# One pass over the weight rows for Q, K and V of an octet, with held stationary rows for K and V

## The chip, the cores and the metric

The kernel runs on one core of a Trainium2 chip. The time is device microseconds of one execution; 2,165.54 us is the median of three runs before (2,163.02 to 2,171.04). Engines are named as in the profile: PE (matrix multiply), with its weight loads on a track of their own (PEld), DVE (vector), ACT (scalar), POOL and SP (SyncE, which only issues transfers here). "Clock" is the share of full speed that PE's clock was granted.

## The reference

Two parts are mixed by a gate. Part B is a gated MLP over 2,048 rows; it takes the first 350 us and the change leaves it alone. Part A is what this case is about: 64 segments of 32 rows, each with 8 memory rows in front, and each segment's memory is the output of the one before, so the segments run one after another.

```python
# D = 640, H = 32 heads of 192, M = 8 memory rows, seg = 32
for s in range(64):
    h = concat([mem, x[s*32:(s+1)*32]])          # 40 rows
    q, k, v = h @ Wq, h @ Wk, h @ Wv             # 640 -> 32 * 192 each
    p = softmax(mask(q @ k.T * 192**-0.5))       # per head
    o = (p @ v) @ Wo                             # 6144 -> 640
    mem = o[:8]; outs.append(o[8:])
return sigmoid(x @ gate_w) * concat(outs) + (1 - ...) * mlp(x)
```

## The kernel before

The weights of part A are 31.5 MB, of which the program keeps 22.6 MB in SBUF beside the rest. They are cut in 84 pieces: for each octet (8 heads, four octets) and each of five 128-row slices k one piece of Q, of K and of V (384 KB each), and 24 pieces of Wo (320 KB). 60 pieces stay in SBUF, 24 are streamed again in every segment through a ring of five slots. A table of costs spreads the streamed pieces evenly over the order in which they are used.

```python
PROG = [("q", 0), ("tq", 0), ("k", 0), ("tk", 0), ("v", 0),
        ("q", 1), ("sc", 0), ("tq", 1), ("k", 1), ("ex", 0), ("tk", 1), ("v", 1),
        ("q", 2), ("pt", 0), ("sc", 1), ("tq", 2), ("k", 2), ("ex", 1), ("tk", 2), ("pv", 0), ("v", 2),
        ("q", 3), ("pt", 1), ("sc", 2), ("tq", 3), ("k", 3), ("ex", 2), ("tk", 3), ("pv", 1), ("v", 3),
        ("wo", 0), ("pt", 2), ("sc", 3), ("ex", 3), ("pv", 2), ("wo", 1), ("wo", 2, 0), ("pt", 3), ("wo", 2, 1),
        ("pv", 3), ("wo", 2, 2), ("wo", 3)]
```

Of a segment's 40 rows the program puts 32 in a column tile of PE (`128*32` in the profile) and leaves out the last 8 positions of x; their Q and K are made for all segments in advance, their V once for four segments. PROG is the order of work of one segment, and each engine follows it with its own instructions: q, k, v are the matmuls with their evictions on ACT (PE writes into the banks of PSUM; an eviction copies a bank to SBUF, and the program lets the bank be written again only then), tq and tk the transposes of Q and K on DVE, sc the scores on PE with maximum and subtraction on DVE, ex the exponentials on ACT with sum, reciprocal and product on DVE, pt the transposes of the probabilities on PE with their evictions on DVE, pv and wo the last two products. Q or K of an octet:

```python
def cmode(s, m, o, bank):
    for k in range(KT):                                   # KT = 5
        g_, rg_ = piece(s, (m, o, k))                     # resident, or the ring slot
        S_.add("pe", [lambda e, j=j, ...: e.matmul(       # loads the 32 rows of H, then 384 columns
            ps[32*j:32*j+32, bank, 0:384]..., Hb[hb][:, k, 0:L], gv[:, j],
            start=(k == 0), stop=(k == KT-1), tile_position=(0, 32*j)) for j in range(4)], ...)
    S_.add("act", ... out=rows_sb[m], in_=ps[:, bank, 0:384] ...)      # "rows evac"
```

V (`v_oct`) has the same form. In every fourth segment (s % 4 == 0) it makes V a second time in the same loop, for the memory positions of the next four segments, into a second PSUM bank that DVE evicts. These are called double-V segments below, the others ordinary ones. Of the eight PSUM banks five (`misc_bank`) are handed out in turn; two are for scores and one for the output. V has two buffers in SBUF (`NVB = 2`).

Of the kernel before, what the change touches and what calls it, by code (L numbers as in the profile page):

```python
# [3 lines left out]
ACTF = mybir.ActivationFunctionType  # L4
# [217 lines left out]
def _build(nc, A_x, A_mem0, A_Wq, A_Wk, A_Wv, A_Wo, seg_len, w_gate, w_up, w_down,  # L222
           gate_w, out, opts=None):
# [5 lines left out]
    L = int(seg_len)  # L229
    assert Bsz == 1 and M == 8 and L == 32 and Dh == 192  # L230
    assert Dm % 128 == 0 and H % 4 == 0 and S % 128 == 0 and Df % 128 == 0
    KT = Dm // 128
# [8 lines left out]
    XA = L - M  # L241
# [15 lines left out]
    S_ = _Sched(nc)  # L257
# [26 lines left out]
    NVB, NUB = 2, 2  # L284
# [34 lines left out]
    ps = nc.alloc_psum_tensor("ps", [128, 8, 512], F32)  # L319
# [5 lines left out]
    o = wsA_base - wsB_total  # L325
# [6 lines left out]
    o = wsA_base  # L332
# [4 lines left out]
    o = ffn_base  # L337
# [14 lines left out]
    Hb = [bview(o_H + b * KT * R * 2, KT * R * 2).rearrange("p (k r) -> p k r", r=R) for b in range(2)]  # L352
    r_Hm = [sreg(o_H + b * KT * R * 2, 8) for b in range(2)]
    r_Hxp = [sreg(o_H + b * KT * R * 2 + 8, KT * R * 2 - 8) for b in range(2)]
    o_Hx = wsA_off["Hx"]
    Hx = bview(o_Hx, KT * 256).rearrange("p (k t) -> p k t", t=128)
    r_Hx = sreg(o_Hx, KT * 256)
# [26 lines left out]
    rows_sb = [bview(wsB_off["rows"] + b * 768, 768) for b in range(2)]  # L384
    r_rows = [sreg(wsB_off["rows"] + b * 768, 768) for b in range(2)]
# [3 lines left out]
    v_sb = [bview(wsB_off["v"] + b * 768, 768) for b in range(NVB)]  # L389
# [69 lines left out]
    def piece_view(key, o):  # L459
        if key[0] == 3:  # L460
            return bview(o, GO).rearrange("p (c n) -> p c n", n=Dm)
        return bview(o, GQ)

    PROG = [("q", 0), ("tq", 0), ("k", 0), ("tk", 0), ("v", 0),
            ("q", 1), ("sc", 0), ("tq", 1), ("k", 1), ("ex", 0), ("tk", 1), ("v", 1),
            ("q", 2), ("pt", 0), ("sc", 1), ("tq", 2), ("k", 2), ("ex", 1), ("tk", 2), ("pv", 0), ("v", 2),
            ("q", 3), ("pt", 1), ("sc", 2), ("tq", 3), ("k", 3), ("ex", 2), ("tk", 3), ("pv", 1), ("v", 3),
            ("wo", 0), ("pt", 2), ("sc", 3), ("ex", 3), ("pv", 2), ("wo", 1), ("wo", 2, 0), ("pt", 3), ("wo", 2, 1),
            ("pv", 3), ("wo", 2, 2), ("wo", 3)]
    assert NOCT == 4  # L470
    WOP = 6
    COST = dict(q=0.17, k=0.17, v=0.2, sc=0.5, pt=0.2, pv=0.5, wo=0.26, tq=0.0, tk=0.0, ex=0.0)

    def wo_pairs(item):
        o_ = item[1]
# [6 lines left out]
    tt = 0.0  # L482
    for item in PROG:
        kind, i = item[0], item[1]
        if kind in ("q", "k", "v"):
            keys = [("qkv".index(kind), i, k) for k in range(KT)]
        elif kind == "wo":
            keys = [(3, p) for p in wo_pairs(item)]
        else:
            tt += COST[kind]  # L490
            continue
        for key in keys:
            order.append(key)
            tcons.append(tt)
            tt += COST[kind]
# [60 lines left out]
    def piece(seg, key):  # L556
        oi = order_index[key]
        assert oi == last_req.get(seg, -1) + 1, "pieces must be consumed in `order`"
        last_req[seg] = oi
        if seg == 0:  # L560
            load_late(oi + LATE)
        if key in res_off:
            assert slot_class[key] != 1 or order_index[key] <= order_index[late[late_done[0] - 1]]
            return piece_view(key, res_off[key]), r_res[key]
        issue_ring(seg, stream_pos[key])
        slot = ring_of[(seg, key)]
        return piece_view(key, ring_off[slot]), r_ring[slot]
# [7 lines left out]
            load_resident(late[late_done[0]])  # L575
            late_done[0] += 1

    left_stream = [order[i] for i in stream_list if order[i][0] < 2]
    left_slot = {}

    def issue_left(upto):
# [278 lines left out]
    def misc_bank():  # L860
        misc[0] += 1
        return misc[0] % 5
# [1 line left out]
    def apx(ap, dims):  # L864
        return bass.AP(ap.tensor, ap.offset, [list(ap.ap[0])] + [list(d) for d in dims])

    def cmode(s, m, o, bank):
        hb = s % 2
        for k in range(KT):
            g_, rg_ = piece(s, (m, o, k))  # L870
            gv = g_.rearrange("p (c j i) -> p j c i", c=12, j=4)
            S_.add("pe", [lambda e, j=j, k=k, gv=gv: e.matmul(  # L872
                ps[32 * j:32 * j + 32, bank, 0:384].rearrange("p (c i) -> p c i", i=32), Hb[hb][:, k, 0:L], gv[:, j],
                start=(k == 0), stop=(k == KT - 1), tile_position=(0, 32 * j)) for j in range(4)],
                reads=[rg_, r_Hm[hb], r_Hxp[hb]], writes=[r_ps[bank]], name="%s s%d o%d k%d" % ("QK"[m], s, o, k))
        S_.add("act", lambda e: e.activation(out=rows_sb[m], in_=ps[:, bank, 0:384], func=ACTF.Copy),  # L876
               reads=[r_ps[bank]], writes=[r_rows[m]], name="rows evac")

    def row_transp(s, m, o):
        src = rows_sb[m].rearrange("p (t c r) -> p t c r", c=3, r=L)  # L880
# [7 lines left out]
        for i, (a, lo) in enumerate(((8, 0), (12, 64))):  # L888
            S_.add("dve", lambda e, a=a, lo=lo: e.transpose(out=Ks[lo:lo + 64, a:a + 4, 0:L], in_=src[lo:lo + 64, :, 1]),  # L889
                   reads=[r_rows[1]], writes=[r_K[1 + i][0]], name="Tk s%d o%d" % (s, o))  # L890

    def v_oct(s, o):
        hb = s % 2
        bank = misc_bank()
        left = s % 4 == 0
        bank2 = misc_bank() if left else None

        def mms(bk, lhs, k, g_):
            return [lambda e, j=j: e.matmul(  # L899
                ps[32 * j:32 * j + 32, bk, 0:384], lhs, g_[:, 384 * j:384 * (j + 1)],  # L900
                start=(k == 0), stop=(k == KT - 1), tile_position=(0, 32 * j)) for j in range(4)]

        for k in range(KT):
            g_, rg_ = piece(s, (2, o, k))
            S_.add("pe", mms(bank, Hb[hb][:, k, 0:L], k, g_),
                   reads=[rg_, r_Hm[hb], r_Hxp[hb]], writes=[r_ps[bank]], name="V s%d o%d k%d" % (s, o, k))
            if left:
                S_.add("pe", mms(bank2, Hx[:, k, 4 * XA:128], k, g_),
                       reads=[rg_, r_Hx], writes=[r_ps[bank2]], name="Vl s%d o%d k%d" % (s, o, k))
        S_.add("act", lambda e: e.activation(out=v_sb[o % NVB], in_=ps[:, bank, 0:384], func=ACTF.Copy),  # L910
               reads=[r_ps[bank]], writes=[r_v[o % NVB]], name="V evac s%d o%d" % (s, o))
        if left:
            S_.add("dve", lambda e: e.tensor_copy(out=vl_sb[o], in_=ps[:, bank2, 0:384]),
                   reads=[r_ps[bank2]], writes=[r_vl[o]], name="Vl evac s%d o%d" % (s, o))

    def scores(s, o):
        bank = 5 + o % 2
# [108 lines left out]
    def segment(s):  # L1026
        g, q = s // 4, s % 4
        for item in PROG:
            kind, i = item[0], item[1]
            if kind in ("q", "k"):  # L1030
                cmode(s, "qk".index(kind), i, misc_bank())
                if kind == "k" and i == 0 and q == 0 and g > 0:
                    out_group(g - 1, misc_bank())
                if kind == "k" and i == 1:
                    if q == 0 and g > 0:
                        out_store(g - 1)
                    if q == 1 and g + 1 < NG:
                        perm_dma(lambda j: rowb[PP[j]], lambda j: rows(x2, g + 1)[j], [], r_rowbh, "rowb")
                    if q == 3 and g + 1 < NG:
                        x_group_transposes(g + 1, misc_bank())  # L1040
                if kind == "k" and i == 2:
                    if s + 1 < NSEG:
                        x_copy(s + 1)
                    if q == 3:
                        if g + 1 < NG:
                            gate_group(g + 1, misc_bank())
                        perm_dma(lambda j: rowb[PP[j]], lambda j: rows(b_scr, g)[j],
                                 [Rg("dr", 128 * g, 128 * g + 128)], r_rowbh, "rowb")
            elif kind == "tq":
                row_transp(s, 0, i)  # L1050
            elif kind == "tk":
                row_transp(s, 1, i)
            elif kind == "sc":
                scores(s, i)
            elif kind == "ex":
                softmax(s, i)
            elif kind == "v":
                v_oct(s, i)
            elif kind == "pt":
                p_transp(s, i)  # L1060
            elif kind == "pv":
                pv_oct(s, i)
            else:
                wo_part(s, item)
        O3 = ps[:, OB, 0:KT * R].rearrange("p (n r) -> p n r", r=R)
        if s + 1 < NSEG:
            nb = (s + 1) % 2
            S_.add("act", lambda e: e.activation(out=Hb[nb][:, :, XA:L], in_=O3[:, :, XA:L], func=ACTF.Copy),
                   reads=[r_ps[OB]], writes=[r_Hm[nb]], name="mem evac s%d" % s)
        S_.add("dve", lambda e: e.tensor_copy(out=aT4[:, :, q * XA:(q + 1) * XA], in_=O3[:, :, 0:XA]),  # L1070
               reads=[r_ps[OB]], writes=[r_aT4], name="aT evac s%d" % s)
        S_.add("dve", lambda e: e.tensor_copy(out=aT4[:, :, 4 * XA + q * M:4 * XA + (q + 1) * M], in_=O3[:, :, L:R]),
               reads=[r_ps[OB]], writes=[r_aT4], name="aT evac2 s%d" % s)
# [86 lines left out]
```

## Time and profile before

| | before |
|---|---|
| time | 2,165.54 us |
| steady part (from 350 us): one segment | 28.7 us |
| double-V segments / ordinary ones | 29.1 / 28.5 us |
| steady part: DMA, PE, DVE busy | 96%, 85%, 63% |
| half-clock time after 360 us | 64 us |

The length of a segment is the distance between two starts of ACT's memory eviction, of which there are 63 (line L1068 in the profile of before). The half-clock time is the sum of the trace's records with a granted clock of 0.5.

The windows view of before: length, then busy us (and instructions) of each engine, the granted clock, the DMA share and GB/s.

```profile
core 0: us, PE busy (x) PEld busy (x) DVE busy (x) ACT busy (x) POOL busy (x), PEclk, DMA share, GB/s
500.00:1000.00 500.00, 424.11 (x10525) 275.76 (x10521) 313.18 (x1042) 148.93 (x372) 74.29 (x329) 0.99 0.96 322
1000.00:1500.00 500.00, 424.78 (x10611) 282.72 (x10608) 315.06 (x1044) 146.70 (x367) 72.11 (x319) 0.98 0.96 320
```

PE is "busy" 85% of the time and DMA 96%, at 322 GB/s. Who ends PE's idle time is told by the waits view of PE, from 362 to 2,100 us: PE's line, what it waited for, us in total, times, the longest.

```profile
PE ps L872 <- DMA arena<-in_A_Wq_dram: 72.9, 121, 1.9
PE ps L992 <- DVE arena L978: 36.2, 96, 0.7
PE ps L1021 <- DVE arena L1008: 33.6, 97, 0.5
PE ps L899 <- DMA arena<-in_A_Wv_dram: 30.2, 48, 1.8
PE ps L1021 <- DMA arena<-in_A_Wo_dram: 29.4, 59, 3.0
```

L872 is Q and K, L899 is V, L1021 is Wo, L992 is PV. Weight pieces of the ring end most of it. Some lines of PE's timeline in an ordinary segment: start, length, instructions, and in brackets the idle time before.

```profile
1043.18 1.81 PE L872 MATMUL ps<-arena 128*32 128x384 bf16 x40 [0.29 <-ACT arena L1068]
1044.82 0.99 PE L899 MATMUL ps<-arena 128*32 128x384 bf16 x20
1045.63 0.99 PE L872 MATMUL ps<-arena 128*32 128x384 bf16 x20
...
1047.84 0.34 PE L899 MATMUL ps<-arena 128*32 128x384 bf16 x4
1049.94 0.35 PE L899 MATMUL ps<-arena 128*32 128x384 bf16 x4 [1.76 <-DMA arena<-in_A_Wv_dram]
```

The 40 matmuls of L872 start at 1043.18 and the next line starts at 1044.82: 1.64 us for 40, 41 ns each, although each has a weight load of its own (40 in the same stretch of PEld's timeline; 96 ns is the mean of one on the page). The bracket in the last line is a piece that came 1.76 us late.

Split by kind of segment, PE's idle time by what ended it (the waits view, one window for each segment; us per segment):

| before | DVE | ACT | DMA | sum |
|---|---|---|---|---|
| double-V segment | 1.49 | 0.30 | 1.05 | 2.84 |
| ordinary segment | 1.27 | 0.30 | 2.87 | 4.44 |

### The profile page before, as it was taken

The numbers are of one execution on the slowest core, as the hardware profiler recorded it, in microseconds if no ns is written. First come the engines' busy times: TensorE is split into PE (matmuls) and PEld (weight loads), VectorE is DVE, ScalarE is ACT, GpSimd is POOL, SyncE is SP. The second block draws the span as 40 slices with busy tenths as digits, with TensorE's granted clock in tenths as the row PEclk, the third lists the DMA queues.
The fourth block names the chain that finished last, engine by engine and source line by source line (L and its number), as shares of the span: only waits on it lengthen the run. The fifth ranks groups of instructions, "written<-read, shape, count | busy, mean of one in ns | idle before, by whom it ended". The sixth has DMA issues, their size and how long they took to land.

```text
span 2166.5 us, 92005 instructions
## 1 busy us (share of the span) xinstructions
PE 1836.7 (85%) x40326; PEld 1154.9 (53%) x40326; DVE 1231.5 (57%) x3952; ACT 618.8 (29%) x1480; POOL 274.1 (13%) x1210
## 2 busy tenths in 40 slices
PE   7999948888888888888888888888888888888887
PEld 3544425555555555555555555555555555555555
DVE  2222316666656566656666666656666666666665
ACT  2222212333232223332322223322323222323232
POOL 0000001111111111111111111111111111111111
PEclk9999979999999999999999999999999999999999
DMA  9203579999999999999999999999999999999998
GB/s 366 103 13 89 149 220 341 328 321 337 322 325 316 310 326 329 313 327 311 329 328 314 324 315 332 323 307 316 334 319 333 320 325 306 328 327 328 322 321 273
DMA packets 363391, 642.97 MB, mean 297 GB/s; under 512 B 60514, under 2 KB 231786, under 8 KB 362986
## 3 DMA queue, kind: packets, MB, share of 16 engines
q1 hardware_dynamic: 311914, 601.41, 81.6%
q10 hardware_dynamic: 51072, 35.66, 5.7%
q8 instruction: 315, 5.16, 0.9%
q14 instruction: 90, 0.74, 0.1%
HBM read 619.13 MB, written 17.83 MB: 294 GB/s over the span
## 4 chain that ended last, share of the span: by engine, by line
DMA 48%; PE 37%; DVE 9%; ACTq 3%; issue 2%; ACT 2%; SPq 0%; POOL 0%; DVEq 0%; POOLq 0%
DMA arena<-in_A_Wq_dram 19%; DMA arena<-in_A_Wo_dram 13%; DMA arena<-in_A_Wv_dram 10%; PE ps L872 9%; PE ps L1021 7%; PE ps L899 5%; DMA arena<-in_A_Wk_dram 4%; PE ps L804 3%; PE ps L742 2%; ACTq L819 2%; PE ps L739 2%; PE ps L757 2%; PE ps L992 2%; DVE arena L975 2%; DVE arena L1008 1%
## 5 line engine op out<-in xcount | busy, mean ns | idle before, releaser
L872 PE MATMUL ps<-arena 128*32 128x384 bf16 x10240 | 566.8, 331 | 119.9 <-DMA arena<-in_A_Wq_dram 77.6
L1021 PE MATMUL ps<-arena 128*128 128x40 bf16 x15360 | 472.1, 181 | 71.7 <-DVE arena L1008 35.9
L1021 PEld LDWEIGHTS ps<-arena 128*128 128x128 bf16 x15360 | 434.9, 97 | 116.8 <-DVE arena L1008 48.0
L872 PEld LDWEIGHTS ps<-arena 128*32 128x32 bf16 x10240 | 239.6, 96 | 346.5 <-DMA arena<-in_A_Wq_dram 172.1
L876 ACT ACTIVATE arena<-ps 128x384 bf16<-128x384 f32 x512 | 251.4, 491 | 552.2 <-PE ps L872 446.8
L899 PE MATMUL ps<-arena 128*32 128x384 bf16 x6400 | 333.1, 331 | 37.0 <-DMA arena<-in_A_Wv_dram 32.2
L835 POOL COPY arena<-arena 128x96 bf16<-128x96 bf16 x256 | 67.6, 264 | 1645.1 <-PE ps L931 1089.0
L899 PEld LDWEIGHTS ps<-arena 128*32 128x32 bf16 x6400 | 150.5, 97 | 175.6 <-DMA arena<-in_A_Wv_dram 82.0
L882 DVE STREAM_TRANSPOSE arena<-arena 128x384 bf16<-128x384 bf16 x256 | 146.0, 570 | 102.3 <-ACT arena L876 102.3
L975 DVE TENSOR_TENSOR arena<-ps,arena 128x320 bf16<-128x320 bf16 x256 | 125.8, 491 | 125.9 <-PE ps L973 121.9
L1002 ACT ACTIVATE arena<-ps 128x320 bf16<-128x320 f32 x256 | 110.7, 432 | 229.4 <-PE ps L994 229.4
L910 ACT ACTIVATE arena<-ps 128x384 bf16<-128x384 f32 x256 | 125.6, 491 | 161.9 <-PE ps L899 161.9
L839 POOL COPY arena<-arena 64x32 bf16<-64x32 bf16 (+1 forms) x768 | 165.7, 216 | 47.3
L959 DVE TENSOR_REDUCE arena<-ps 104x4 f32<-104x160 f32 x256 | 82.6, 323 | 150.6 <-ACT ps L957 148.6
L992 PE MATMUL ps<-arena 128*128 128x160 bf16 (+1 forms) x768 | 133.7, 264 | 39.6 <-DVE arena L978 38.0
L889 DVE STREAM_TRANSPOSE arena<-arena 64x128 bf16<-64x128 bf16 x512 | 145.5, 284 | 8.1
L957 ACT ACTIVATE ps<-ps 104x160 f32<-104x160 f32 x256 | 74.0, 289 | 233.9 <-DVE ps L947 189.0
L994 PE MATMUL ps<-arena 128*128 128x64 bf16 (+1 forms) x768 | 128.0, 206 | 2.1 <-DMA arena<-in_A_Wv_dram 1.0
L945 DVE TENSOR_REDUCE arena<-ps 104x4 f32<-104x160 f32 x256 | 81.0, 316 | 77.0 <-PE ps L931 77.0
L885 DVE STREAM_TRANSPOSE arena<-arena 128x256 bf16<-128x256 bf16 x256 | 111.4, 435 | 16.1 <-ACT arena L876 16.1
L992 PEld LDWEIGHTS ps<-arena 128*128 128x128 bf16 x768 | 73.9, 99 | 85.5 <-DVE arena L978 60.3
L1006 DVE CAST arena<-ps 64x160 bf16<-64x160 f32 x256 | 80.4, 314 | 52.5 <-PE ps L994 48.4
(79 smaller groups left out, 1719.8 us busy)
## 6 DMA issues: line engine op xcount, KB each, us to landing
arena<-in_A_Wo_dram SPq DMA_DIRECT2D x591, 320.0 KB, 4.9
arena<-in_A_Wq_dram SPq DMA_DIRECT2D x404, 384.0 KB, 5.3
arena<-in_A_Wv_dram SPq DMA_DIRECT2D x335, 384.0 KB, 5.1
arena<-in_A_Wk_dram SPq DMA_DIRECT2D x276, 384.0 KB, 5.3
left_qk_scratch<-arena ACTq DMA_DIRECT2D x16, 768.0 KB, 8.8
arena<-left_qk_scratch ACTq DMA_DIRECT2D x64, 192.0 KB, 4.5
arena<-in_A_x_dram SPq DMA_DIRECT2D x4, 640.0 KB, 15.1
ffn_b_scratch<-arena ACTq DMA_DIRECT2D x16, 160.0 KB, 1.8
```

What stands on the lines that cost most here:

```text
L839: S_.add("pool", lambda e, a=a, b=b, lo=lo, hi=hi, sa=sa: e.tensor_copy(out=Ks[lo:hi, a:b, L:R], in_=stg[lo:hi, o, 1, sa:sa + b - a]), rea ...
L872: S_.add("pe", [lambda e, j=j, k=k, gv=gv: e.matmul(ps[32 * j:32 * j + 32, bank, 0:384].rearrange("p (c i) -> p c i", i=32), Hb[hb][:, k, ...
L876: S_.add("act", lambda e: e.activation(out=rows_sb[m], in_=ps[:, bank, 0:384], func=ACTF.Copy), reads=[r_ps[bank]], writes=[r_rows[m]], na ...
L882: S_.add("dve", lambda e: e.transpose(out=Qs[:, :, 0:L], in_=rows_sb[0].rearrange("p (c r) -> p c r", r=L)), reads=[r_rows[0]], writes=[r_ ...
L885: S_.add("dve", lambda e: e.transpose(out=apx(Ks[:, 0, :], [[2 * R, 4], [R, 2], [1, L]]), in_=apx(rows_sb[1], [[96, 4], [64, 2], [1, L]])) ...
L889: S_.add("dve", lambda e, a=a, lo=lo: e.transpose(out=Ks[lo:lo + 64, a:a + 4, 0:L], in_=src[lo:lo + 64, :, 1]), reads=[r_rows[1]], writes= ...
L899: return [lambda e, j=j: e.matmul(ps[32 * j:32 * j + 32, bk, 0:384], lhs, g_[:, 384 * j:384 * (j + 1)], start=(k == 0), stop=(k == KT - 1) ...
L910: S_.add("act", lambda e: e.activation(out=v_sb[o % NVB], in_=ps[:, bank, 0:384], func=ACTF.Copy), reads=[r_ps[bank]], writes=[r_v[o % NVB ...
L975: S_.add("dve", lambda e: e.tensor_tensor(out=PTm, in0=apx(pv[:, 512:616], [[64, 2], [0, 4], [1, R]]), in1=apx(mbd, [[0, 2], [1, 4], [0, R]]),
L992: return [lambda e: e.matmul(full, v[:, e0:e0 + 128], PTm[:, ia:ib], start=True, stop=False, skip_group_check=True), lambda e: e.matmul(pa ...
L994: lambda e: e.matmul(part, vl[:, e0:e0 + 128], PTl[:, ia:ib], start=False, stop=True, skip_group_check=True)]
L1021: fns.append(lambda e, g_=g_, i=i, c=c, n=n, tl=tl, cc=cc, u=u: e.matmul(ps[:, OB, n * R:(n + 1) * R], g_[:, i, n * 128:(n + 1) * 128], u[ ...
```

## The change

Its intent: Q, K and V multiply the same 32 rows of H, so for each slice k the rows are loaded for Q only and K's and V's matmuls run on the rows that are in the array (`ldweights=False`). For that Q, K and V of an octet become one item, `qkv`, with k outermost; V's slice 0 comes last, so that V's bank is needed a little later. V's eviction becomes an item of its own, `ve`. The place of scores, of the softmax relative to K's transposes, and of the Wo pieces changes with it.

```diff
-    PROG = [("q", 0), ("tq", 0), ("k", 0), ("tk", 0), ("v", 0),
-            ("q", 1), ("sc", 0), ("tq", 1), ("k", 1), ("ex", 0), ("tk", 1), ("v", 1),
-            ...
-            ("wo", 0), ("pt", 2), ("sc", 3), ("ex", 3), ("pv", 2), ("wo", 1), ("wo", 2, 0), ("pt", 3), ("wo", 2, 1),
-            ("pv", 3), ("wo", 2, 2), ("wo", 3)]
+    PROG = [("qkv", 0), ("tq", 0), ("tk", 0), ("ve", 0),
+            ("qkv", 1), ("sc", 0), ("tq", 1), ("tk", 1), ("ex", 0), ("ve", 1),
+            ("qkv", 2), ("pt", 0), ("sc", 1), ("tq", 2), ("tk", 2), ("ex", 1), ("pv", 0), ("ve", 2),
+            ("qkv", 3), ("pt", 1), ("sc", 2), ("tq", 3), ("tk", 3), ("ex", 2), ("pv", 1), ("ve", 3),
+            ("wo", 0, 0), ("sc", 3), ("wo", 0, 1), ("pt", 2), ("ex", 3), ("wo", 0, 2), ("pv", 2),
+            ("wo", 1, 0), ("wo", 1, 1), ("pt", 3), ("wo", 1, 2), ("pv", 3), ("wo", 2), ("wo", 3)]
+    QKV = [(m, k) for k in range(KT) for m in range(3) if (m, k) != (2, 0)] + [(2, 0)]
...
+    def qkv_oct(s, o):
+        left = s % 4 == 0                                        # double-V segment
+        banks = [misc_bank() for _ in range(3)]
+        bank2 = misc_bank() if left else None
+        load_k = [None]
+        for m, k in QKV:
+            load = load_k[0] != k
+            load_k[0] = k
...                                                               # four matmuls, with or without load
+            if left and m == 2:
+                S_.add("pe", mms(bank2, Hx[:, k, 4 * XA:128], True), ...)     # second V
+                load_k[0] = None
+        for m in range(2): ...                                   # "rows evac" of Q and K on ACT
...
+    def v_evac(s, o):                                            # at the item "ve"
+        S_.add("act", ... out=v_sb[o % NVB], in_=ps[:, bank, 0:384] ...)
+        if bank2 is not None:
+            S_.add("dve", ... out=vl_sb[o], in_=ps[:, bank2, 0:384] ...)
```

Of the 16,640 loads for these matmuls 9,216 go. Since the streamed pieces are chosen from the order of use, the choice changes too: 14 of Q, K, V and 10 of Wo in place of 15 and 9.

## The prediction

> **What bounds it now.** After about 350 us the kernel repeats 64 recurrent segments, 28.7 us each (ACT's 63 memory evictions, 353.1 to 2130.9 us). In windows of 500 us DMA is 96% busy there at 320 to 324 GB/s, PE 85%, DVE 63%. A segment streams 24 weight pieces through a ring of five slots (15 of Q, K, V, 384 KB each; 9 of Wo, 320 KB), some 5 us each from issue to landing. SyncE waits for slots that PE frees, and PE for pieces: 146 us of PE idle time from 362 to 2100 us, 317 us on PE's load track (waits view). So the ring sets the pace, with DVE's chain (about 4.4 us an octet) close behind. Every fourth segment makes V twice (3.3 us more PE work), yet is only some 0.7 us longer: most PE time is hidden.
>
> **What the removed loads are worth: nothing.** In unbroken stretches 40 matmuls of Q and K start in 1.64 us (timeline): 41 ns each, 164 ns for four 384-column matmuls side by side. [...]the loads (97 ns each) are hidden. [...] Some 9,200 loads vanish; the matmuls stay 41 ns apart.
>
> **What moves.** The plan becomes 14 Q/K/V and 10 Wo pieces a segment, 8,576 KB instead of 8,640. At this trace's packet times (140 ns per 3,072 bytes, 63 ns per 1,280) that is 0.3% less DMA time, 5 us in all.
> Q, K and V end together after 15 groups (2.46 us); the first scores, and the DVE chain, come some 1.5 us later in a segment. In return DVE has Q's and K's transposes (1.6 us) to do during the exponentials, for which it waits 149 us now. Three PSUM banks are held at once, and V's eviction goes behind the exponentials and the PV eviction on ACT: octet 3's V meets octet 2's V bank, about 0.8 us of new PE wait. In the 16 double-V segments four of the five banks are held, and the second V's DVE eviction stands behind the mix (0.35 + 0.88 us) and the transposes: by hand some 2 us of PE wait in octet 1, 1 in octet 2, 3 in octet 3. Scores 3 waits about 1 us for K's transposes.
>
> **Sum.** An ordinary segment: chain about 1 us longer by hand, mostly under the DMA pace, some given back by the hidden exponentials: -0.5 to +0.5 us, times 48. A double-V segment: +2 to +4 us, times 16, about +45 us. DMA -5 us. I predict 2,200 us (+1.6%), 8 in 10 between 2,130 and 2,270. Faster by over 2%: 0.12; within 2%: 0.46; slower by over 2%: 0.42.
>
> **Right or wrong by.** Q/K/V matmuls still 41 ns apart; PE idle before them ended by V's evictions (ACT, DVE) more than by DMA; double-V segments 31 to 33 us, others near 28.5; steady DMA share 0.93 to 0.95; DVE's wait for exponentials clearly under 149 us.
>
> **What would make it wrong.** Held matmuls closer than 41 ns. DMA waits that absorb the bank waits as they absorb the second V now (then about 2,165). An order of pieces that feeds the ring better, towards the 375 GB/s seen around 330 to 340 us: 2 to 4% faster. Waits behind V's evictions that compound through the ring: 5% slower.

16 times +2 to +4 us was put at about +45, 48 times -0.5 to +0.5 at 0, DMA is -5, so +40 us on 2,165.5, put as 2,200. What stands there "by hand", the later start of scores and the 4.4 us of DVE's chain are estimates from instruction times of the trace of before (63% of 28.7 us, by four, gives 4.5). The 375 GB/s is 378 in the windows view of 330 to 340 us.

## The result, and the profile after

The changed kernel takes 2,360.68 us (median of four runs, 2,355.45 to 2,372.38); the kernel before took 2,164.28 on the same chip. The ratio is 1.0894 (95% interval 1.0839 to 1.095). All ratios here are the mean time of one kernel's fast runs over that of the kernel before in the same rounds, so they are not quite the ratios of the medians. The prediction was 2,200 us, at most 2,270.

The windows view of after, as above:

```profile
core 0: us, PE busy (x) PEld busy (x) DVE busy (x) ACT busy (x) POOL busy (x), PEclk, DMA share, GB/s
500.00:1000.00 500.00, 395.65 (x9576) 216.32 (x7333) 274.11 (x932) 125.17 (x332) 64.67 (x287) 0.92 0.88 287
1000.00:1500.00 500.00, 395.05 (x9570) 218.03 (x7339) 278.85 (x948) 125.61 (x334) 66.13 (x294) 0.92 0.88 287
```

DMA fell from 96% to 88% and from 320 to 287 GB/s, PE from 85% to 79%, and the granted clock from 0.98 to 0.92. No engine is busier. The last part can be seen on the page itself. First the page of before, its granted clock and DMA share in 40 slices of the span, in tenths; then the page of after.

```profile
PEclk9999979999999999999999999999999999999999
DMA  9203579999999999999999999999999999999998
```

```profile
PEclk9999979999998999998998998999998899999989
DMA  9104599899898989898989889898988898989888
```

The half-clock records sum to 279 us after 360 us, against 64. PE's waits view of after, from 362 to 2,300 us (L873 are matmuls on held rows, L898 those with a load, L1014 is PV, L919 and L922 are V's eviction on ACT and the second V's on DVE):

```profile
PE ps L1014 <- DVE arena L1000: 129.0, 207, 1.6
PE ps L873 <- DMA arena<-in_A_Wk_dram: 36.8, 51, 1.7
PE ps L898 <- DVE arena L922: 29.1, 15, 2.0
PE ps L942 <- DVE arena L935: 28.9, 42, 0.7
...
PE ps L873 <- ACT arena L919: 27.8, 48, 1.1
...
PE ps L873 <- DVE arena L922: 26.9, 15, 1.8
...
PE ps L898 <- ACT arena L919: 8.7, 15, 0.6
```

Four of these seven lines are waits for V's evictions, 92.5 us together; the kernel before has none of them. PV waits 129 us for DVE, 36 before. By kind of segment, PE's idle time by what ended it (the waits view, one window for each segment; us per segment):

| | length, us | PE idle: DVE | ACT | DMA | sum |
|---|---|---|---|---|---|
| double-V, before | 29.1 | 1.49 | 0.30 | 1.05 | 2.84 |
| double-V, after | 37.9 | 6.91 | 1.70 | 0.52 | 9.13 |
| ordinary, before | 28.5 | 1.27 | 0.30 | 2.87 | 4.44 |
| ordinary, after | 29.75 | 2.69 | 0.64 | 2.41 | 5.74 |

A double-V segment became 8.8 us longer, an ordinary one 1.2 us: 16 times 8.8 and 48 times 1.2 are 198 us, all of the loss. One double-V segment on PE's timeline (it starts at 953.7 us):

```profile
954.45 0.50 PE L873 MATMUL ps<-arena 128*32 128x384 bf16 x8
954.78 0.50 PE L898 MATMUL ps<-arena 128*32 128x384 bf16 x8
...
958.71 0.50 PE L873 MATMUL ps<-arena 128*32 128x384 bf16 x8
961.18 0.51 PE L898 MATMUL ps<-arena 128*32 128x384 bf16 x8 [1.97 <-DVE arena L922]
...
964.60 0.50 PE L873 MATMUL ps<-arena 128*32 128x384 bf16 x8
965.68 0.51 PE L898 MATMUL ps<-arena 128*32 128x384 bf16 x8 [0.58 <-ACT arena L919]
...
969.78 0.35 PE L898 MATMUL ps<-arena 128*32 128x384 bf16 x4
970.92 0.33 PE L873 MATMUL ps<-arena 128*32 128x384 bf16 x4 [0.80 <-ACT arena L919]
...
973.37 0.33 PE L873 MATMUL ps<-arena 128*32 128x384 bf16 x4 [1.79 <-DVE arena L922]
...
974.30 0.86 PE L898 MATMUL ps<-arena 128*32 128x384 bf16 x8
974.94 0.86 PE L873 MATMUL ps<-arena 128*32 128x384 bf16 x8
...
984.07 0.24 PE L1014 MATMUL ps<-arena 128*128 128x160 bf16 x1 [1.57 <-DVE arena L1000]
```

The first two lines give the pace: eight matmuls with held rows start at 954.45 and the next item at 954.78, 0.33 us, so again 41 ns each. Then come the waits: 1.97 us in octet 1 (second V's bank), 0.58 in octet 2 (V's bank), 0.80 and 1.79 in octet 3, and 1.57 before the PV of octet 2. Behind the waits of octet 3 the pace is half (the trace's record from 974.04 to 977.45 us has a granted clock of 0.5): the item that starts at 974.30 is followed at 974.94, eight matmuls in 0.64 us. What DVE does while PE waits in octet 1:

```profile
958.32 0.88 DVE L851 SCALAR_TENSOR_TENSOR arena<-ps,arena 128x640 bf16<-128x640 bf16 x1 [3.50 <-PE ps L846]
959.12 0.57 DVE L928 STREAM_TRANSPOSE arena<-arena 128x384 bf16<-128x384 bf16 x1
959.61 0.40 DVE L931 STREAM_TRANSPOSE arena<-arena 128x256 bf16<-128x256 bf16 x1
959.93 0.60 DVE L935 STREAM_TRANSPOSE arena<-arena 64x128 bf16<-64x128 bf16 x2
960.57 0.56 DVE L922 CAST arena<-ps 128x384 bf16<-128x384 f32 x1
```

The mix of the group before, Q's transposes, K's transposes, and only then the second V's eviction (L922), which ends at 961.13. PE goes on at 961.18.

### The profile page after: what moved, and what is told of

It is laid out like the page before. It is cut to its first block, busy times and chain, and to the rows that moved or that the text cites. A ratio compares the mean times of both kernels' runs of the same rounds, so it can differ in the third digit from the quotient of the medians.

```text
span 2353.6 us, 82743 instructions
## 1 busy us (share of the span) xinstructions
PE 1874.9 (80%) x40298; PEld 1001.3 (43%) x31110; DVE 1204.0 (51%) x3952; ACT 588.1 (25%) x1480; POOL 273.6 (12%) x1210
## 5 line engine op out<-in xcount | busy, mean ns | idle before, releaser
L873 PE MATMUL ps<-arena 128*32 128x384 bf16 x9216 | 640.8, 340 | 136.2 <-DMA arena<-in_A_Wk_dram 37.0
L898 PE MATMUL ps<-arena 128*32 128x384 bf16 x7424 | 598.8, 345 | 122.0 <-DMA arena<-in_A_Wv_dram 30.6
L898 PEld LDWEIGHTS ps<-arena 128*32 128x32 bf16 x7424 | 202.8, 99 | 867.4 <-issue 481.9
L1043 PEld LDWEIGHTS ps<-arena 128*128 128x128 bf16 x15360 | 458.9, 99 | 27.1 <-DMA arena<-in_A_Wo_dram 7.4
L911 ACT ACTIVATE arena<-ps 128x384 bf16<-128x384 f32 x512 | 223.2, 488 | 701.8 <-PE ps L898 602.6
L1014 PE MATMUL ps<-arena 128*128 128x160 bf16 (+1 forms) x768 | 147.6, 282 | 140.1 <-DVE arena L1000 135.6
L967 DVE TENSOR_REDUCE arena<-ps 104x4 f32<-104x160 f32 x256 | 81.6, 319 | 147.4 <-PE ps L953 145.9
L1014 PEld LDWEIGHTS ps<-arena 128*128 128x128 bf16 x768 | 79.2, 106 | 166.7 <-DVE arena L1000 166.7
L1016 PE MATMUL ps<-arena 128*128 128x64 bf16 (+1 forms) x768 | 139.7, 219 | 2.2 <-DMA arena<-in_A_Wq_dram 1.9
L919 ACT ACTIVATE arena<-ps 128x384 bf16<-128x384 f32 x256 | 125.8, 491 | 10.9 <-PE ps L898 10.4
L805 PE MATMUL ps<-arena 128*128 128x512 bf16 x470 | 105.3, 383 | 6.5 <-ACT arena L812 6.0
L1092 DVE CAST arena<-ps 128x120 bf16<-128x120 f32 x64 | 18.1, 283 | 177.7 <-ACT arena L1090 172.3
L953 PE MATMUL ps<-arena 128*40 128x40 bf16 x4096 | 96.7, 180 | 13.0 <-DVE arena L935 13.0
```

The lines of the kernel that those rows point to most:

```text
L873: return e.add_instruction(ins)
L898: fns.append(lambda e, j=j, out=out, rhs=rhs: e.matmul(out, lhs, rhs, start=first, stop=last, tile_position=(0, 32 * j)))
L911: S_.add("act", lambda e, m=m: e.activation(out=rows_sb[m], in_=ps[:, banks[m], 0:384], func=ACTF.Copy), reads=[r_ps[banks[m]]], writes=[r ...
L919: S_.add("act", lambda e: e.activation(out=v_sb[o % NVB], in_=ps[:, bank, 0:384], func=ACTF.Copy), reads=[r_ps[bank]], writes=[r_v[o % NVB ...
L1014: return [lambda e: e.matmul(full, v[:, e0:e0 + 128], PTm[:, ia:ib], start=True, stop=False, skip_group_check=True), lambda e: e.matmul(pa ...
L1016: lambda e: e.matmul(part, vl[:, e0:e0 + 128], PTl[:, ia:ib], start=False, stop=True, skip_group_check=True)]
```

## The experiments

All ran on one core, all were correct; each ratio is to the kernel before on the same chip. "W" is the theory that PE's waits for V's PSUM banks make most of the loss, with the halved clock behind them. The rivals: matmuls on held rows are slow; the new choice of pieces feeds the ring worse; the later scores or the new order of the Wo part delay DVE's chain.

| run | edit | median us | ratio (95%) | double-V / ordinary, us | half clock, us |
|---|---|---|---|---|---|
| after | the change | 2,360.7 | 1.0894 (1.0839 to 1.0950) | 37.9 / 29.75 | 279 |
| a1_all_loads | after, all loads | 2,347.7 | 1.0832 (1.0753 to 1.0911) | 37.9 / 29.6 | 225 |
| a2_early_v | after, V evicted early | 2,259.9 | 1.0421 (1.0359 to 1.0482) | 30.6 / 30.1 | 272 |
| a3_dummies | after, fill the waits (flawed) | 2,379.6 | 1.0975 (1.0904 to 1.1047) | 39.0 / 29.8 | 223 |
| a5_dummies2 | the same, mended | 2,348.2 | 1.0841 (1.0801 to 1.0881) | 36.0 / 29.95 | 210 |
| a4_tail | a2, old Wo order | 2,228.3 | 1.0299 (1.0260 to 1.0338) | 30.1 / 29.5 | 164 |
| a6_pv_inside | a4, PV inside the pass | 2,217.0 | 1.0228 (1.0196 to 1.0261) | 30.0 / 29.4 | 168 |
| a7_early_sc | a6, scores 0 earlier | 2,236.2 | 1.0337 (1.0306 to 1.0368) | 31.2 / 29.3 | 189 |
| a8_ex_first | a6, old DVE order | 2,218.2 | 1.0231 (1.0177 to 1.0285) | 30.4 / 29.2 | 183 |
| a9_in_turn | a6, no one pass | 2,223.0 | 1.0262 (1.0209 to 1.0314) | 30.6 / 29.2 | 176 |
| b1_plan | before, after's pieces | 2,237.4 | 1.0317 (1.0255 to 1.0380) | 30.5 / 29.5 | 117 |
| b3_even | before, 14 + 10, even | 2,177.8 | 1.0052 (0.9997 to 1.0107) | 29.6 / 28.7 | 92 |
| b2_tail | before, after's Wo order | 2,172.6 | 1.0037 (1.0003 to 1.0072) | 28.9 / 28.7 | 47 |
| b4_late_sc | before, scores 0 later | 2,305.9 | 1.0659 (1.0606 to 1.0712) | 31.2 / 30.7 | 206 |
| d1_half | before, half a piece resident | 2,157.7 | 0.9967 (0.9935 to 0.9999) | 29.1 / 28.5 | 74 |
| d2_half_tk | d1, K's transposes first | 2,167.5 | 0.9987 (0.9923 to 1.0051) | 28.9 / 28.6 | 88 |

### The loads alone

```diff
-            load = load_k[0] != k
+            load = True
```

> The changed kernel with every Q, K and V matmul loading its stationary rows again; nothing else differs. If loads are hidden and worth nothing (theory: waits for V's banks make the loss), the time is that of the changed kernel, 2,350 to 2,370 us, ratio to before 1.08 to 1.10, and 384-column matmuls stay 41 ns apart. Rival: matmuls on held rows are themselves slower or stall PE; then this run is clearly faster, toward 2,165 to 2,250 us. If the held rows did help, it is slower than 2,400 us.

1.0832, against 1.0894 with held rows; the intervals overlap widely. From PE's timeline of this run, an unbroken stretch with loads (L898):

```profile
943.39 1.81 PE L898 MATMUL ps<-arena 128*32 128x384 bf16 x40 [0.99 <-DMA arena<-in_A_Wq_dram]
945.13 0.45 PE L846 MATMUL ps<-arena 128*128 128x128 bf16 x5
```

40 matmuls with their loads take 1.81 us to the end of the last, exactly as the 40 of the kernel before at 1043.18. At this pace held rows are neither slower nor faster. (All four times of this run lie below all four of the changed kernel, by 13 us at the medians, with 225 us of half clock in place of 279; the ratios do not tell this from nothing.) The rival falls, and so does the change's own reason.

### V's evictions early

```diff
-    NVB, NUB = 2, 2
+    NVB, NUB = 3, 2
...
         vbanks[o] = (banks[2], bank2)
+        v_evac(s, o)                     # right behind Q's and K's "rows evac"; the item "ve" does nothing
...
-            S_.add("dve", lambda e: e.tensor_copy(out=vl_sb[o], ...
+            S_.add("act", lambda e: e.activation(out=vl_sb[o], ..., func=ACTF.Copy),
```

> The changed kernel with V's and the second V's evictions moved to ACT right behind Q's and K's (a third V buffer of 768 bytes makes that legal; the plan of pieces stays). If PE's waits for V's PSUM banks make most of the loss, the double-V segments fall from 37.9 us to 31 to 33, ordinary ones from 29.75 to about 29, half-clock time from 279 us to under 150, the whole to 2,180 to 2,260 us. If the loss comes from the plan of pieces, the later scores or the Wo order, the time stays above 2,310 us.

100 us of the 196 go: 1.0894 to 1.0421. All of it comes from the double-V segments (37.9 to 30.6 us); ordinary ones became 0.3 us longer (30.1). PE's waits view of this run, from 362 to 2,100 us, its longest lines:

```profile
PE ps L1015 <- DVE arena L1001: 97.1, 162, 1.1
PE ps L898 <- DMA arena<-in_A_Wq_dram: 40.7, 57, 1.9
PE ps L873 <- DMA arena<-in_A_Wk_dram: 37.5, 42, 2.2
```

The lines for V's evictions are gone from the list. The expectation was right for the total (at its upper edge), a little too cautious for double-V segments (31 to 33 us expected), and wrong for ordinary segments (29 us expected) and for the half clock, which stayed at 272 us and moved: 34 us of it are in double-V segments now, the rest in the others, mostly 22 to 28 us into the segment, in the Wo part. The run moves V's and the second V's evictions together and does not tell them apart.

### The clock behind the waits

```diff
             if left and m == 2:
+                if k == order_v[0] and o in (1, 3):
+                    S_.add("pe", [lambda e: e.matmul(ps[:, OB, 256:512]..., ident, Hx[:, 0:2, :], ...) for _ in range(14)], ...)
                 S_.add("pe", mms(bank2, ...                      # second V
```

> The changed kernel with 14 unneeded matmuls (128 by 256, about 1.5 us) in each of the two long waits of PE in a double-V segment (octets 1 and 3); they fit into the waits, so they lengthen nothing by themselves. If the clock that halves after those waits costs real time on top of the waits, the half-clock time of double-V segments (116 us of 16) falls by half or more and the whole gets 15 to 45 us faster, 2,315 to 2,345 us. If the half clock lies under other waits, the time stays within 10 us of the changed kernel, or is longer.

The 1.5 us are an estimate: 14 times 256 columns at the 164 ns that 384 columns took in the trace of before are 1.53 us.

This failed by its placing. In octet 3 PE's 1.8 us wait is ahead of V's slice 1, and the unneeded matmuls stood behind it: they ran at half clock and took 3.17 us (the timeline of that run), on top of the wait. The mended run puts those of octet 3 ahead of V's slice 1 and loads V's rows again:

```diff
+            if left and m == 2 and k == order_v[0] and o == 3:
+                ...                                               # the same 14 matmuls
+                load_k[0] = None
             load = load_k[0] != k
```

> The run with unneeded matmuls, mended: in the first try those of octet 3 stood behind the wait that they were to fill (1.8 us, ahead of V's k 1) and so lengthened the segment. Now they stand ahead of it; those of octet 1 as before. If the clock that halves after these waits has a price of its own: half clock in double-V segments falls from 116 us (16 segments) to under 60, these segments get 1 to 3 us shorter (37.9 to 35 to 37), the whole 2,310 to 2,345 us. If not: within 10 us of 2,360 us.

Its timeline in octets 1 and 3 of a double-V segment (L914 and L885 are the unneeded matmuls):

```profile
954.52 1.70 PE L914 MATMUL ps<-arena 128*128 128x256 bf16 x14
956.56 0.51 PE L904 MATMUL ps<-arena 128*32 128x384 bf16 x8 [0.34 <-DVE arena L933]
...
966.63 0.33 PE L873 MATMUL ps<-arena 128*32 128x384 bf16 x4
966.89 1.70 PE L885 MATMUL ps<-arena 128*128 128x256 bf16 x14
968.76 0.67 PE L904 MATMUL ps<-arena 128*32 128x384 bf16 x12 [0.16 <-DVE arena L933]
969.25 0.50 PE L873 MATMUL ps<-arena 128*32 128x384 bf16 x8
969.58 0.50 PE L904 MATMUL ps<-arena 128*32 128x384 bf16 x8
```

The matmuls fill the waits (0.34 and 0.16 us are left of 1.97 and 1.79), and behind them the pace is 0.33 us for eight. In double-V segments the half clock fell from 116 to 55 us (of the 15 that lie between two memory evictions) and their length from 37.9 to 36.0 us (means of 15 segments, standard errors 0.4 and 0.2). So the halved clock has a price of its own, some 1.9 us in each, about 30 us in all by this view. In the total it shows as 1.0894 to 1.0841, with intervals that overlap, the median of 2,348 lies just outside the expected range, and the run with all loads, without unneeded matmuls, had 1.0832: on the total alone this would not be settled. From the trace of after an estimate can be had another way: the matmul spacings within half-clock records, less those of like matmuls at full clock, sum to some 50 to 70 us, by what is counted as like, and to some 10 us in the trace of before.

### The choice of pieces

```diff
+    streamed = set(order.index(key) for key in [...])             # the kernel before with a fixed list
```

> The kernel before with the changed kernel's set of streamed pieces (14 of Q, K, V and 10 of Wo) and nothing else of the change. If the plan is harmless, 2,150 to 2,185 us, ratio 0.99 to 1.01. Rival: the new set feeds the ring worse (DMA share fell from 0.96 to 0.88); then this run is slower by several per cent, 2,230 us or more.

1.0317: the rival seemed to hold. But the list was even in the changed kernel's order of use; in the order of before it has gaps from 0.34 to 2.56 on the program's own scale of time, where its own list has 0.51 to 1.46. So the same numbers of pieces were tried at even distances:

> The kernel before with 14 pieces of Q, K, V and 10 of Wo like the changed kernel, but chosen at even distances in its own order of use (gaps 0.5 to 1.5 in the program's own time scale; in the earlier run with the changed kernel's set they were 0.3 to 2.6). If uneven distances made that run 3.2% slower, this one is within 1% of before, 2,145 to 2,190 us. If ten Wo pieces are worse than nine, it is again 2,210 us or more.

1.0052 (0.9997 to 1.0107). Ten Wo pieces cost at most 1%; the distances made the rest. The first of the two runs therefore says nothing of the change, but much about this ring: the same bytes at uneven distances cost 2.6%.

### The order of the Wo part

```diff
-            ("wo", 0, 0), ("sc", 3), ("wo", 0, 1), ("pt", 2), ("ex", 3), ("wo", 0, 2), ("pv", 2), ...
+            ("wo", 0), ("pt", 2), ("sc", 3), ("ex", 3), ("pv", 2), ("wo", 1), ("wo", 2, 0), ...
```

> The kernel with early V evictions (2,260 us) with the Wo part of the program in the order of the kernel before (probability transposes ahead of scores 3, so the PV of octet 2 no longer waits on DVE behind the maximum and subtraction of octet 3). If the waits in the Wo phase and the halved clock that follows them (272 us of half clock, most of it 22 to 28 us into a segment) are the second part of the loss: the wait of the PV matmuls for DVE falls from 97 us to about 40, half clock to under 130 us, the time to 2,190 to 2,225 us. If the later start of the DVE chain or the plan of pieces is what is left, it stays within 1% of 2,260 us.

1.0421 to 1.0299, 32 us, and half clock 272 to 164 us. The direction is as expected, but the time just misses its range and the half clock misses by more (under 130 us expected); the wait of PV for DVE fell only from 97 to 84 us, not to 40, and 45 us of waits for the last step of the softmax came new. The other way round, the new Wo order in the kernel before:

> The kernel before with nothing of the change but its order of the Wo part (the same 24 pieces streamed). If that order by itself makes new PE waits and half clock: 2,190 to 2,230 us and half clock of 120 us or more (64 before). If it is harmless without the rest of the change: 2,150 to 2,185 us.

1.0037: harmless. Of these two kernels the order costs time only in the one where DVE's chain already runs late (32 us there, 0.4% here).

### What is left

> The kernel with early V evictions and the old Wo order (2,228 us), with the PV matmuls of octet 0 put inside the pass of octet 3 in ordinary segments, and those of octet 1 behind two pieces of Wo, so that PE has matmuls to run while DVE evicts the transposed probabilities. If what is left of the loss is that a pass in one piece leaves PE nothing to fill DVE's latency with: PE's waits for DVE in ordinary segments fall from about 2.8 us to 1.5 to 2.1, the time to 2,180 to 2,210 us. If it is the later start of scores and of DVE's chain, the waits move to other places and the time stays within 0.7% of 2,228 us.

```diff
         for m, k in QKV:
+            if not left and o == 3 and (m, k) == (0, 2):
+                pv_oct(s, 0)                 # was behind scores 1, ahead of the pass
+                load_k[0] = None
...
-            ("wo", 0), ("pt", 2), ...
+            ("wo", 0, 0), ("pv", 1), ("wo", 0, 1), ("wo", 0, 2), ("pt", 2), ...
```

1.0228. PE's waits for DVE in ordinary segments fell from 2.84 to 2.19 us, the time by 11 us: both miss what was expected, and the time is within the 0.7% that the expectation gave to its rival (the waits move). Three runs went for the rest.

> The best form of the changed kernel so far (2,217 us) with two changes in octets 0 and 1: octet 0's Q and K in the first ten groups and its V behind them, and the scores of octet 0 inside the pass of octet 1 (after nine of 15 groups) instead of behind it. That lets DVE's chain start about 1 us earlier in each segment. If the late start is the rest of the loss: 2,160 to 2,190 us. If it is not, within 0.7% of 2,217 us.

The 1 us is an estimate: six groups at the 164 ns of the trace of before.

```diff
+    QKV0 = [(m, k) for k in range(KT) for m in range(2)] + [(2, k) for k in range(KT)]      # octet 0
+            if o == 1 and (m, k) == (0, 3):
+                scores(s, 0)
```

1.0337, slower than without, and outside both expected ranges. Ordinary segments gained nothing (29.4 to 29.3 us), double-V segments lost 1.2 us, with PE waiting 0.4 us more for DVE and 0.3 us more for DMA in each. What exactly stands against the earlier scores there was not followed up.

> The best form of the changed kernel so far (2,217 us, PV inside the pass) with the softmax of the octet before put ahead of K's transposes on DVE again, as in the kernel before (the change had put it behind them). PE's waits for the softmax's last step are 55 us there and 5 us in the kernel before. If the later probabilities are the rest of the loss: those waits fall under 20 us and the time to 2,165 to 2,200 us, although DVE then waits for the exponentials again (over 80 us). If they only move to the scores, which then wait for K's transposes: within 0.7% of 2,217 us.

```diff
-            ("qkv", 2), ..., ("tq", 2), ("tk", 2), ("ex", 1), ...          # and so in octets 1 and 3
+            ("qkv", 2), ..., ("tq", 2), ("ex", 1), ("tk", 2), ...
```

1.0231. The waits for the softmax fell from 55 to 13 us as foreseen, others grew (PV for DVE 54 to 71, scores for K's transposes from under 2 to 17), and the time stood still.

> The best form of the changed kernel (2,217 us) with the one pass itself undone: Q, K and V of an octet one after another again, each with its own loads, in the same place of the program (scores still behind the whole octet). If the simultaneous end of Q, K and V makes the rest of the loss: 2,170 to 2,200 us. If the place of scores, transposes and PV between the matmuls makes it, which stays as it is: within 0.7% of 2,217 us.

```diff
-    QKV = [(m, k) for k in range(KT) for m in range(3) if (m, k) != (2, 0)] + [(2, 0)]
+    QKV = [(m, k) for m in range(3) for k in range(KT)]
```

1.0262, no different from 1.0228. With this the one pass itself is gone, with all loads back, and the loss of some 50 us stays. What then still differs from the kernel before is above all where scores, transposes and PV stand: between whole octets, not between Q, K and V. (The ten Wo pieces, V's evictions and its third buffer differ too; of these only the pieces were tried in the kernel before.) How much that can cost was asked of the kernel before:

```diff
-            ("q", 1), ("sc", 0), ("tq", 1), ("k", 1), ("ex", 0), ("tk", 1), ("v", 1),
+            ("q", 1), ("k", 1), ("v", 1), ("sc", 0), ("tq", 1), ("tk", 1), ("ex", 0),
```

> The other way round: the kernel before, the same streamed pieces, with octet 0's scores (and octet 1's transposes behind them) moved from behind Q of octet 1 to behind K and V of octet 1, 10 groups or 1.64 us of matmuls later. If a later start of DVE's chain costs what it moves, less what DVE makes good: 0.6 to 1.2 us a segment, 2,200 to 2,245 us. If PE and the ring absorb it: within 0.7% of before.

1.0659, 142 us or 2.2 us a segment for scores that stand 1.64 us of matmuls later, twice what was expected. PE's waits view of this run, from 362 to 2,100 us (L967 is the softmax's last step):

```profile
PE ps L875 <- DVE arena L967: 83.9, 47, 2.3
PE ps L975 <- DVE arena L967: 23.2, 17, 1.7
```

These 107 us were 6 in the kernel before. A reading that fits: K and V of octet 1 no longer lie between octet 0's scores and its probabilities, so PE also runs out of work there. The edit also puts octet 1's transposes of K ahead of octet 0's softmax on DVE; a run below does that in three octets of the kernel before, beside half a piece kept resident, and has 0.9987 (0.9967 without it).

### A try at a faster version

> A try at beating both, from the theory that ring bytes and DVE's chain set the pace of the kernel before: half of one streamed V piece (rows of octet 1, k 1) is kept in 1,536 free bytes, 2.2% fewer bytes a segment, and K's transposes stand ahead of the softmax of the octet before on DVE, so that DVE does not wait for the exponentials (136 us in the steady part). If the theory holds: 2,105 to 2,150 us, DVE's wait for exponentials under 30 us. If the pace is set elsewhere: within 0.7% of before.

```diff
+    HK = (2, 1, 1)          # this V piece: columns 0 to 767 resident, 768 to 1535 streamed
-            ("k", 1), ("ex", 0), ("tk", 1), ...
+            ("k", 1), ("tk", 1), ("ex", 0), ...
```

0.9987. DVE's waits for the exponentials fell from 136 to 39 us, not under 30, and nothing was gained. Without the second edit:

> The kernel before with half of one streamed V piece kept resident, and no change of order: 2.2% fewer streamed bytes, one of 24 loads half as long. If the ring's bytes set the pace (DMA 96% busy): 1 to 2% faster, 2,120 to 2,145 us. If the pace is set by when slots come free, within 0.5% of before.

0.9967 (0.9935 to 0.9999): perhaps 0.3%, for 2.2% fewer streamed bytes. DMA is busy 96% of the time, yet bytes are not what the time hangs on.

## Why the prediction was wrong

Right:
- The loads were worth nothing. 41 ns a matmul before, after, and with all loads put back. To each 164 ns of matmuls there are four loads of 96 ns (means of the page of before), and the pace is the same without them. In the timelines of before the loads of L899 start at 1044.66, while the 40 matmuls of L872 run to 1044.99 and L899's own start at 1044.82.
- The waits by hand. For double-V segments the text has 2, 1 and 3 us in octets 1, 2 and 3. The timeline has 1.97, 0.58, and 0.80 + 1.79 us, with the releasers named. For ordinary segments it has "chain about 1 us longer"; they became 1.2 us longer, but this match is in part luck: some 0.6 us of it went with the new Wo order (30.1 to 29.5 us when that was undone), which the text did not count.
- DVE's wait for the exponentials, 136 us in the steady part of before, is absent from DVE's waits after. It was worth nothing: DVE's wait for PE's transposes of the probabilities grew from 114 to 210 us (its waits views, 362 to 2,100 us).

Wrong:
- The step that failed is the discount in "Sum": "+2 to +4 us" for a double-V segment after 6 us of waits, and "-0.5 to +0.5 us" for an ordinary one, "mostly under the DMA pace". The measured terms are +8.8 and +1.2 us. The argument was that 3.3 us of the second V's matmuls already hide in a double-V segment. But that had used the room up: PE's wait for DMA in such a segment was 1.05 us before, and it fell to 0.52; the new waits for DVE and ACT are 6.8 us. In ordinary segments 2.87 us of DMA wait stood there to absorb, and only 0.46 of it did. While PE waits for a bank it frees no ring slot, so DMA idles as well: SyncE, which waits for slots, waited 1,246 us in all for PE from 362 to 2,100 us (1,143 before), at the longest 4.2 us (2.3 before), and the DMA share fell to 0.88 (0.93 to 0.95 predicted). With the waits undiscounted the same sum would have been 16 times 6 and 48 times 1, less 5: +139 us. Measured, PE's idle time grew by 6.3 and 1.3 us a segment, 163 us in all.
- The clock was not in the prediction at all. Behind waits of 1 to 2 us PE ran at half clock for 279 us in place of 64. The longest idle time of PE in its waits view of after is 2.0 us. In the 3.41 us ahead of a half-clock record PE idled 1.6 us at the median (1.0 to 2.5), but other such stretches with as much idle time were not followed by one, so no rule is drawn here. Of the 74 half-clock records 66 last 3.41 us, seven 6.83 and one 6.15. The price of the half clock is an estimate: some 30 us by the mended run, in double-V segments alone, and 40 to 60 us by the spacings. PE's idle time leaves 33 of the 196 us over, in which PE was not idle but took longer; that is of this size.
- "Scores 3 waits about 1 us" was right (0.69 us in the timeline of that segment), but the text missed that the new Wo order also puts octet 3's maximum and subtraction ahead of octet 2's evictions on DVE (1.57 us before PV). This and its half clock were 32 us.
- One of its own checks failed: PE's idle time before Q, K and V was to be ended by V's evictions more than by DMA. It was 92.5 us against 111 us of DMA waits. The last line of the text, waits behind V's evictions "that compound through the ring", had named the failure, at 5% and as the less likely case; it was 9%.

What stays open: about 50 us of the ratio 1.0228. Of that, up to 1% may be the ten Wo pieces. In the best form of the changed kernel PE waits 2.42 us a segment for DVE and 2.65 for DMA, 1.32 and 2.43 in the kernel before. That they come from the place of scores and PV among the matmuls is argued from what remains after undoing the rest, and not shown. Moving scores in the kernel before shows that it can cost more than this, but putting octet 0's scores earlier in the changed kernel gained nothing; which of the moves makes which part stays open.

## What to carry to other kernels

Before loads are saved, compare the pace of an unbroken run of matmuls with and without them: where it is the same, saving them may buy nothing (41 ns each here, and ratios of 1.0894 with held rows and 1.0832 with all loads). Count the PSUM banks that the new order holds at once and follow each eviction through its engine's queue; and take a new wait off against idle time only where that stage of the same segment still has some, since a wait of the engine that frees ring slots can hold up the transfers too (here DMA fell from 96% to 88%, while SyncE's waits for PE grew from 1,143 to 1,246 us). When an order of work is made coarser, latencies that the old order filled with other matmuls can come into the open (PV's wait for DVE, 36 to 129 us here), and the clock may fall with it (0.98 to 0.92 here).
